# Retention followed by two expert layers on one Trainium2 core: program order on four more queues, decays per chunk, keys scaled on ScalarE

## The chip, the cores and the metric

The kernel runs on one core of a Trainium2 chip. The metric is the device time of one execution in microseconds (us); less is better. A kernel's time is the median of several executions.

## The reference

Retention over 4 batches of 8 heads, 576 positions, head size 64, followed by two dense layers over the 2304 tokens:

```python
scores = scale * np.matmul(q, k.transpose(0, 1, 3, 2))
gamma = 1.0 - 2.0 ** (-5.0 - np.arange(H, dtype=np.float32))
Dmat = np.where(rel >= 0, gamma[:, None, None] ** rel[None, :, :], 0.0)   # rel = query pos - key pos
attn = np.matmul(scores * Dmat[None], v)          # then heads joined: x is 2304 x 512
g = x @ w_gate                                    # 512 x 1536
x = (g * sigmoid(g) * (x @ w_val)) @ w_out        # first layer
h = np.maximum(x @ w_in, 0.0)                     # 512 x 2048
return (h * h) @ w_out2                           # second layer
```

The weights arrive as float64 and are converted on the core.

## The kernel before, in words

**Stage 1, retention.** Two heads make a pair; there are 16 pairs (`pairs`, batch by batch, four a batch). The sequence of a pair is cut into chunks of 128 positions (four whole ones and one of 64). Within a chunk the scores are computed directly (`scores`: matmuls into PSUM tile `s`, then VectorE multiplies them with `mask_sb` into `p_sb`, and for the last short chunk into `pl`). Between chunks a state is carried (`states`: scaled keys times values into PSUM tile `kvs`; ScalarE copies the first chunk's, VectorE adds the other three up, into `sb`). `prep_state` makes the scaled keys in place in `kv_sb` (VectorE for pairs 0 to 3, GpSimd after that) and the scaled queries `qs` (GpSimd). `apply` multiplies states and scores with queries and values into PSUM (`o` for four chunks, a part of the tile `s` for the last), and ScalarE copies that to `xy`. `load` fetches queries and keys (`qk_sb`, three buffers) and values and keys (`kv_sb`, four buffers), and in the first four pairs a quarter each of the mask and of the query decays `qs_sb`.

A loop of 18 steps (n = 0 to 17) runs this as a pipeline: step n computes `scores` and `states` of pair n and, LAG = 2 steps late, `apply` of pair n - 2. The calls stand in the order load(n+2), prep_state(n+1), scores, apply for four chunks, scores of the last chunk, states, one call of `hidden1_early` in steps 6 to 17, apply for the last chunk.

**Work between the steps.** From step 3 on, five calls of `pump` a step advance the conversion of the weights by one piece each. A unit of weights (128 x 512) is loaded as float64 into one of two `raw` buffers (`prefetch`); its five pieces are two ScalarE operations (L161, L162), a clamp (L164), then for the unit before it the split into a high and a low part (`w_hi` on ScalarE, `w_lo` on VectorE, L145 and L146) with a shift (L168), a merge (L170) and an addition (L179). `split_x` cuts 512 columns of `xy` into a high part `xh` (ScalarE) and a low part `xl` (VectorE). `hidden1_early` multiplies the first 512 tokens with one unit (12 matmuls of 512 columns).

**Stage 2** is the rest of both layers: matmuls of 512 columns from `hidden1`, `hidden2`, `out1`, `out2`, three for each product (high x high, high x low, low x high), with the remaining units converted beside them.

**Order.** In stage 1 the matmuls are chained (`tc.issue_after`), so that TensorE runs them in the order of the source. The instructions of VectorE, ScalarE, GpSimd and the DMA triggers on SyncE are put in order by the framework's scheduler, by its own estimate of when each is ready. In stage 2 the scheduler orders all engines.

Of the kernel before, what the change touches and what calls it, by code (L numbers as in the profile page):

```python
# [40 lines left out]
WA = 20  # L41
# [14 lines left out]
def retention_moe_kernel(  # L56
# [34 lines left out]
    chain = {"on": False, "last": None}  # L91

    def matmul(*args, **kw):

        with ExitStack() as behind:
            if chain["on"] and chain["last"] is not None:
                behind.enter_context(tc.issue_after(chain["last"]))
            m = nc.tensor.matmul(*args, **kw)  # L98
        if chain["on"]:
            chain["last"] = m.ins  # L100
        return m
# [10 lines left out]
    def prefetch(upto):  # L112

        while loads["next"] <= min(upto, len(order) - 1):
            i = loads["next"]
            if loads["pool"] < 2:
                loads["pool"] += 1
                raw_flat[i] = raw_p.tile([P, 1024], U32, tag="raw", name="raw")
                raw, back = raw_flat[i].rearrange("p (a n) -> p a n", a=2), None
            elif spare:  # L120
                back = spare.pop(0)
                raw = back.bitcast(U32)
            else:
# [4 lines left out]
            nc.sync.dma_start(out=raw, in_=src.rearrange("p (a n) -> p a n", a=2))  # L128
            raw_t[i] = raw, back
# [12 lines left out]
    def parts_unit(i):  # L142
        wf = w_t.pop(i).bitcast(F32)
        hi, lo = weight_tiles()
        nc.scalar.copy(hi, wf)  # L145
        nc.vector.tensor_tensor(out=lo, in0=wf, in1=f32(hi), op=ALU.subtract)  # L146
        units[order[i]] = (hi, lo)

    def conversion():
        ts = nc.vector.tensor_scalar  # L150
        for i in range(len(order)):
# [9 lines left out]
            nc.scalar.activation(out=low, in_=low16, func=AF.Copy, scale=2.0**-13)  # L161
            nc.scalar.activation(out=wf, in_=high.bitcast(F32), func=AF.Abs)  # L162
# [7 lines left out]
            nc.vector.scalar_tensor_tensor(  # L170
# [7 lines left out]
            for to, lo in adds:  # L178
                nc.vector.tensor_tensor(out=to, in0=to, in1=lo, op=ALU.add)  # L179
# [35 lines left out]
    def split_x(ph, n, cc):  # L215
# [9 lines left out]
        nc.scalar.copy(hi, src)  # L225
        nc.vector.tensor_tensor(out=lo, in0=src, in1=f32(hi), op=ALU.subtract)
        xs[ph, n, cc] = (hi, lo)

    def three(dst, a, b, first, last):
        (ah, al), (bh, bl) = a, b  # L230
        matmul(dst, ah, bh, start=first, stop=False)
        matmul(dst, ah, bl, start=False, stop=False)
        matmul(dst, al, bh, start=False, stop=last)
# [23 lines left out]
    def halves(key, t, early=False):  # L257
# [6 lines left out]
        nc.scalar.copy(hi, t)  # L264
        nc.vector.tensor_tensor(out=lo, in0=t, in1=f32(hi), op=ALU.subtract)  # L265
        hs[key] = (hi, lo)

    def hidden1(n, f, then=None):
# [13 lines left out]
    def hidden1_early(k):  # L282

        f, what = k // 2, "gv"[k % 2]
        if k == 0:
            for cc in range(CC):
                split_x(1, 0, cc)
        (ps,) = project(1, 0, f, (what, what))
        if what == "g":
            early_t[f] = t = t_p.tile([P, 512], F32, tag="t", name="t")  # L290
            nc.scalar.activation(out=t, in_=ps, func=AF.Sigmoid)
        t = early_t[f]
        nc.vector.tensor_tensor(out=t, in0=ps, in1=t, op=ALU.mult)
        if what == "v":
            halves((1, 0, f), early_t.pop(f), early=True)
        if k == 2 * HALF - 1:
            for cc in range(CC):
                split_x(1, 1, cc)

    def hidden2(n, f):  # L300
# [16 lines left out]
    def out1(n, f):  # L317
# [14 lines left out]
        for cc, a in enumerate(acc.pop((1, n))):  # L332
# [5 lines left out]
            if n == 0 and f0:  # L338
                nc.vector.tensor_tensor(out=dst, in0=a[:, :m], in1=dst, op=ALU.add)
            elif cc % 2:  # L340
                nc.vector.tensor_copy(dst, a[:, :m])
            else:
                nc.scalar.copy(dst, a[:, :m])
            if n == 0 and f0 == 0:
                nc.sync.dma_start(out=part[:, cc, :], in_=dst)

    def out2(n, f):
# [7 lines left out]
        if f == F2 - 1:  # L355
            for tt, a in enumerate(acc.pop((2, n))):
# [13 lines left out]
    with ExitStack() as st:  # L370
# [13 lines left out]
        def warm():  # L384

            one = const.tile([P, 256], F32, tag="one", name="one")
            nc.vector.memset(one, 1.0)
            ps = bank("g")
            for _ in range(WARM):
                matmul(ps[:, :256], one[:, :P], one, start=True, stop=True)  # L390

        def load(n):
# [3 lines left out]
            dma = nc.sync.dma_start  # L396
            at = slice(0, CUT) if n == 0 else slice(0, S)
            dma(out=qk_t[n][:, :, at], in_=qk[b, hp][:, :, at])
            if n == 0:
                dma(out=ks_sb, in_=kscale)  # L400
                dma(out=qk_t[n][:, :, CUT:], in_=qk[b, hp][:, :, CUT:])
            dma(out=kv_t[n], in_=kv[b, hp])
            if n < NP:
                dma(out=mask_sb[:, n], in_=mask[:, n])
                dma(out=qs_sb[:, n], in_=qscale[:, n])
# [18 lines left out]
        for x in range(3):  # L424
            nc.gpsimd.memset(p_last[x][S - (NC - 1) * P:], 0.0)

        def scores(n, cs):
# [11 lines left out]
            nc.vector.tensor_tensor(  # L439
# [6 lines left out]
        def states(n):  # L446
# [10 lines left out]
            nc.scalar.copy(sb[:, 0], ps[:, 0])  # L457
            for c in range(1, NC - 1):
                nc.vector.tensor_tensor(out=sb[:, c], in0=ps[:, c], in1=sb[:, c - 1], op=ALU.add)

        def apply(n, last):
# [26 lines left out]
            nc.scalar.copy(xy[:, hp, t0:t0 + bank.shape[-1]], bank)  # L488
# [56 lines left out]
    for ph, n, f, end in steps:  # L545
# [9 lines left out]
        if (ph, n, f) == (1, 0, HALF + 1):  # L555
            nc.sync.dma_start(out=xy[:, :, CHUNKS[1][0][0]:][:, :, :CHUNKS[1][0][1]], in_=part)
# [70 lines left out]
```

## Time and profile before

| | |
|---|---|
| three runs | 951.22, 953.1, 954.19 us; median 953.1 |
| profiled execution | 950.97 us, span 949.2 us |
| mean granted TensorE clock | 0.986 of full speed |
| TensorE busy | 923.5 us, 97% of the span |
| VectorE, ScalarE, GpSimd busy | 469.0, 328.1, 33.7 us |
| moved by DMA | 63.6 MB, mean 67 GB/s |

The span is the time from the first to the last instruction of the profiled execution. Engines are called PE (TensorE), PEld (its weight loads), DVE (VectorE), ACT (ScalarE), POOL (GpSimd), SP (SyncE; SPq its DMA triggers). Because all matmuls go through one helper, they share the line L98, and are told apart by their tiles.

### The profile page before, as it was taken

To read this page: it belongs to the slowest core of one execution; us is meant where nothing else is said; L and a number is where in the kernel's file an instruction comes from. 1 tells how busy PE (TensorE), PEld (TensorE's weight loads), DVE (VectorE), ACT (ScalarE), POOL (GpSimd) and SP (SyncE) were. 2 spreads that over 40 slices of the span, in tenths; PEclk is the share of its full clock that TensorE was granted. 3 is DMA by queue.
4 is the path that set the end of the run, shared out by engine and by line. 5 is a ranking of instruction groups with operands and counts; after the bars stand their busy time and mean duration, and the time that the engine had idled before them with its cause. 6 is when DMAs were issued, how large, how long until landed. Compare 5 with 4: busy or idle time off the path is not lost.

```text
span 949.2 us, 12499 instructions
## 1 busy us (share of the span) xinstructions
PE 923.5 (97%) x5144; PEld 771.5 (81%) x5144; DVE 469.0 (49%) x849; ACT 328.1 (35%) x597; POOL 33.7 (4%) x35
## 2 busy tenths in 40 slices
PE   8499999999999999999999999999999999999998
PEld 6377778788888998888888888888888888888897
DVE  3858667798423332223799888233224222322232
ACT  1443444564312121112566565232223222322232
POOL 2133300000000000000000000000000000000000
PEclk7799999999999999999999999999999999999999
DMA  8756524442100000000244321001001000100010
GB/s 336 248 186 208 197 89 136 137 150 95 60 1 1 2 1 1 1 1 25 69 132 143 122 89 44 1 1 45 1 1 44 1 1 1 45 0 1 1 45 23
DMA packets 22025, 63.60 MB, mean 67 GB/s; under 512 B 2256, under 2 KB 3792, under 8 KB 21968
## 3 DMA queue, kind: packets, MB, share of 16 engines
q1 hardware_dynamic: 21968, 62.81, 19.8%
q8 instruction: 40, 0.66, 0.3%
q14 instruction: 17, 0.14, 0.0%
HBM read 57.03 MB, written 5.77 MB: 66 GB/s over the span
## 4 chain that ended last, share of the span: by engine, by line
PE 81%; DMA 8%; DVE 7%; ACT 2%; issue 1%; SPq 1%; ACTq 0%; DVEq 0%
PE a L98 34%; PE v L98 23%; PE g L98 23%; DMA raw<-in_w 6%; DVE w L170 1%; DVE w L179 1%; DVE w_lo L146 1%; DMA qk_sb<-in_qk 1%; DVE w L164 1%; DMA part<-part_sb 1%; ACT raw L161 1%; DVE p_sb L439 1%; DVE w L168 1%; DVE w_lo L265 0%; ACT w L162 0%
## 5 line engine op out<-in xcount | busy, mean ns | idle before, releaser
L265 DVE TENSOR_TENSOR h_lo<-t,h_hi 128x512 fp32r<-128x512 f32 (+1 forms) x134 | 85.1, 635 | 67.1 <-ACT h_hi L264 66.7
L264 ACT CAST h_hi<-t 128x512 fp32r<-128x512 f32 (+1 forms) x134 | 77.2, 576 | 118.1 <-DVE t L276 64.5
L98 PE MATMUL g<-xh,w_hi 128*128 128x512 f32 (+1 forms) x304 | 114.1, 375 | 0.8 <-ACT xh L225 0.8
L98 PE MATMUL v<-xh,w_hi 128*128 128x512 f32 (+1 forms) x304 | 113.7, 375 | 0.0
L98 PE MATMUL g<-xh,w_lo 128*128 128x512 f32 (+1 forms) x304 | 113.3, 373 | 0.0
L98 PE MATMUL g<-xl,w_hi 128*128 128x512 f32 (+1 forms) x304 | 113.2, 372 | 0.0
L98 PE MATMUL v<-xh,w_lo 128*128 128x512 f32 (+1 forms) x304 | 113.2, 372 | 0.0
L98 PE MATMUL v<-xl,w_hi 128*128 128x512 f32 (+1 forms) x304 | 113.2, 372 | 0.0
L98 PE MATMUL a<-w_lo,h_hi 128*128 128x512 f32 x288 | 112.3, 390 | 0.0
L98 PE MATMUL a<-w_hi,h_hi 128*128 128x512 f32 x288 | 112.2, 390 | 0.0
L98 PE MATMUL a<-w_hi,h_lo 128*128 128x512 f32 x288 | 109.8, 389 | 0.0
L98 PE MATMUL a<-h_lo,w_hi 128*128 128x512 f32 (+1 forms) x216 | 78.9, 366 | 0.0
L98 PE MATMUL a<-h_hi,w_lo 128*128 128x512 f32 (+1 forms) x216 | 78.9, 365 | 0.0
L98 PE MATMUL a<-h_hi,w_hi 128*128 128x512 f32 (+1 forms) x216 | 77.0, 366 | 1.2 <-ACT h_hi L264 1.2
L306 DVE SCALAR_TENSOR_TENSOR t<-g,t 128x512 f32<-128x512 f32 (+1 forms) x40 | 25.5, 637 | 105.5 <-ACT t L304 105.4
L274 DVE TENSOR_TENSOR t<-g,t 128x512 f32<-128x512 f32 (+1 forms) x54 | 34.0, 630 | 85.1 <-ACT t L272 84.8
L306 DVE SCALAR_TENSOR_TENSOR t<-v,t 128x512 f32<-128x512 f32 (+1 forms) x40 | 25.5, 638 | 92.4 <-ACT t L304 92.1
L98 PEld LDWEIGHTS g<-xh,w_hi 128*128 128x128 f32 x304 | 57.2, 188 | 11.5 <-ACT xh L225 1.2
L98 PEld LDWEIGHTS v<-xh,w_hi 128*128 128x128 f32 x304 | 57.3, 188 | 10.3 <-issue 0.2
L98 PEld LDWEIGHTS g<-xh,w_lo 128*128 128x128 f32 x304 | 57.3, 188 | 10.1
L98 PEld LDWEIGHTS v<-xh,w_lo 128*128 128x128 f32 x304 | 57.3, 188 | 10.1
L98 PEld LDWEIGHTS g<-xl,w_hi 128*128 128x128 f32 x304 | 57.3, 188 | 9.8
(88 smaller groups left out, 1486.0 us busy)
## 6 DMA issues: line engine op xcount, KB each, us to landing
raw<-in_w SPq DMA_DIRECT2D x51, 512.0 KB, 3.6
kv_sb<-in_kv SPq DMA_DIRECT2D x16, 576.0 KB, 5.0
xy<-in_w SPq DMA_DIRECT2D x17, 512.0 KB, 3.8
qk_sb<-in_qk SPq DMA_DIRECT2D x15, 576.0 KB, 5.0
out<-o_sb SPq DMA_DIRECT2D x18, 256.0 KB, 2.3
part<-part_sb SPq DMA_DIRECT2D x4, 256.0 KB, 2.8
xy<-part SPq DMA_DIRECT2D x1, 1024.0 KB, 5.3
qs_sb<-in_qscale SPq DMA_DIRECT2D x4, 224.0 KB, 7.4
```

The source lines that it names most:

```text
L98: m = nc.tensor.matmul(*args, **kw)
L146: nc.vector.tensor_tensor(out=lo, in0=wf, in1=f32(hi), op=ALU.subtract)
L161: nc.scalar.activation(out=low, in_=low16, func=AF.Copy, scale=2.0**-13)
L164: ts(out=wf, in0=wf, scalar1=TINY, scalar2=HUGE, op0=ALU.max, op1=ALU.min)
L168: ts(out=w, in0=w, scalar1=3, scalar2=0x3FFFFFFF, op0=ALU.logical_shift_left, op1=ALU.bitwise_and)
L170: nc.vector.scalar_tensor_tensor(out=w, in0=high, scalar=0xC0000000, in1=w, op0=ALU.bitwise_and, op1=ALU.bitwise_or)
L179: nc.vector.tensor_tensor(out=to, in0=to, in1=lo, op=ALU.add)
L264: nc.scalar.copy(hi, t)
L265: nc.vector.tensor_tensor(out=lo, in0=t, in1=f32(hi), op=ALU.subtract)
L274: nc.vector.tensor_tensor(out=t, in0=g, in1=t, op=ALU.mult)
L306: nc.vector.scalar_tensor_tensor(out=t, in0=ps, scalar=0.0, in1=t, op0=ALU.max, op1=ALU.mult)
L439: nc.vector.tensor_tensor(out=pt[:w], in0=ps[:w, :, :nx * w].rearrange("p h (c q) -> p h c q", c=nx), in1=mask_sb[:w, hp, :, None, :w].to_ ...
```

## The change

1. **Order.** A small class `Chained` wraps each of the five engines. While `chain["on"]` holds, that is in stage 1, each instruction on VectorE, ScalarE, GpSimd and each DMA trigger on SyncE is put behind the one before it in the source, as matmuls were already.
2. **The step rewritten.** `load` becomes `load_qk` and `load_kv`. Step n begins with load_kv(n+1) (before: n+2) and load_qk(n+2). `prep_state(n+1)` moves to the end of the step. Two of the five pumps stand together after the main scores (in step 3 only one), and one stands between the last chunk's scores and `states`. `split_x(1, 0, cc)` moves from step 6 to one call in each of steps 3 to 6, between `apply` and the last chunk's scores; `split_x(1, 1, cc)` moves from step 17's `hidden1_early` to after the loop.
3. **Decays per chunk.** Keys are scaled with the decays within one chunk, the same for all chunks; the carried state is multiplied with one decay for each chunk (`scalar_tensor_tensor` in place of `tensor_tensor`). The query decays then repeat too, so `qs_sb` has 161 columns instead of 448, and the GpSimd multiplication is cut into one of 3 x 128 columns and one of 64.
4. **Key scaling on ScalarE**: two `act.mul` of 256 columns a pair with a scale from `ks_sb`, in place of one VectorE or GpSimd multiplication of 512.
5. **WA** goes from 20 to 21: one more weight unit is converted in stage 1 (15 instead of 14).

The core of the diff (all other hunks only replace `nc.vector`, `nc.scalar`, `nc.gpsimd`, `nc.sync` and `matmul` by `dve`, `act`, `pool_e`, `sp` and `pe.matmul`):

```diff
-WA = 20
+WA = 21
...
+        def __getattr__(self, name):
+            op = getattr(self.engine, name)
+
+            def traced(*args, **kw):
+                with ExitStack() as behind:
+                    if chain["on"] and self.last is not None:
+                        behind.enter_context(tc.issue_after(self.last))
+                    i = op(*args, **kw)
+                if chain["on"]:
+                    self.last = i.ins
+                return i
...
+    pe, dve, act, pool_e, sp = map(Chained, (nc.tensor, nc.vector, nc.scalar, nc.gpsimd, nc.sync))
...
-        if k == 0:
-            for cc in range(CC):
-                split_x(1, 0, cc)
...
-        if k == 2 * HALF - 1:
-            for cc in range(CC):
-                split_x(1, 1, cc)
...
-            kn = kv_t[n][:, NC:, :].rearrange("p t (h d) -> p t h d", h=2)
-            (nc.gpsimd if n >= NP else nc.vector).tensor_tensor(
-                out=kn, in0=kn, in1=ks_sb[:, hp].to_broadcast([P, NC - 1, 2, D]), op=ALU.mult
-            )
+            for h, r in enumerate(rs):
+                kn = kv_t[n][:, NC:, r]
+                act.mul(kn, kn, ks_sb[:, hp, 1, h])
             qs = q_p.tile([P, S - P], F32, tag="qs", name="qs")
-            nc.gpsimd.tensor_tensor(
-                out=qs, in0=qk_t[n][:, 0, P:], in1=qs_sb[:, hp, :], op=ALU.mult
-            )
+            for c, m in ((0, 3 * P), (3 * P, D)):
+                w = min(m, P)
+                pool_e.tensor_tensor(
+                    out=qs[:, c:c + m].rearrange("p (c q) -> p c q", q=w),
+                    in0=qk_t[n][:, 0, P + c:P + c + m].rearrange("p (c q) -> p c q", q=w),
+                    in1=qs_sb[:, hp, None, :w].to_broadcast([P, m // w, w]), op=ALU.mult,
+                )
...
-                nc.vector.tensor_tensor(out=sb[:, c], in0=ps[:, c], in1=sb[:, c - 1], op=ALU.add)
+                dve.scalar_tensor_tensor(
+                    out=sb[:, c], in0=sb[:, c - 1], scalar=qs_sb[:, pairs[n][1], -1:], in1=ps[:, c],
+                    op0=ALU.mult, op1=ALU.add,
+                )
...
-        qs_sb = const.tile([P, NP, S - P], F32, tag="qs", name="qs_sb")
-        load(0)
-        load(1)
+
+        qs_sb = const.tile([P, NP, P + D // 2 + 1], F32, tag="qs", name="qs_sb")
+        load_qk(0)
+        load_kv(0)
+        load_qk(1)
         prep_state(0)
...
+            if nxt:
+                load_kv(n + 1)
             if n + 2 <= last:
-                load(n + 2)
+                load_qk(n + 2)
             if n == FROM - 3:
                 prefetch(1)
-            if nxt:
-                prep_state(n + 1)
             if new:
                 scores(n, range(NC - 1))
-            pump(fill)
+            pump(fill if n == FROM - 3 else 2 * fill)
             if old:
                 apply(n - LAG, False)
             pump(fill)
+            if LAG < n <= LAG + CC:
+                split_x(1, 0, n - LAG - 1)
             if new:
                 scores(n, (NC - 1,))
+            pump(fill)
+            if new:
                 states(n)
             pump(fill)
             if FROM <= n < FROM + 2 * HALF:
                 hidden1_early(n - FROM)
-            pump(fill)
             if old:
                 apply(n - LAG, True)
-            pump(fill)
-
+            if nxt:
+                prep_state(n + 1)
+        for cc in range(CC):
+            split_x(1, 1, cc)
     chain["on"] = False
```

## Rows read from the trace of the kernel before

**Rows 1.** The page: busy time of the engines, and one DMA group.

```profile
PE 923.5 (97%) x5144; PEld 771.5 (81%) x5144; DVE 469.0 (49%) x849; ACT 328.1 (35%) x597; POOL 33.7 (4%) x35
...
qs_sb<-in_qscale SPq DMA_DIRECT2D x4, 224.0 KB, 7.4
```

**Rows 2.** Windows by stage: busy us (and instructions) of each engine, clock, DMA share, GB/s.

```profile
4.90:20.82 15.92, 12.54 (x146) 10.44 (x145) 8.32 (x17) 1.63 (x4) 3.40 (x3) 0.68 1.01 389
20.82:32.14 11.32, 4.82 (x77) 3.77 (x73) 8.21 (x18) 5.58 (x12) 2.46 (x3) 0.86 0.76 273
32.14:44.21 12.07, 6.44 (x74) 5.23 (x72) 10.84 (x21) 6.41 (x13) 2.20 (x3) 0.78 0.73 257
...
58.93:66.20 7.27, 7.27 (x89) 5.76 (x85) 3.30 (x7) 1.13 (x4) 2.18 (x3) 1.00 0.51 166
...
137.63:186.00 48.37, 46.41 (x206) 37.80 (x203) 34.81 (x65) 25.42 (x45) 0.00 (x0) 1.00 0.44 134
186.00:944.00 758.00, 757.95 (x3637) 639.78 (x3636) 341.41 (x605) 250.68 (x442) 0.00 (x0) 1.00 0.11 36
```

**Rows 3.** TensorE's waits in the first 270 us: total, times, longest.

```profile
PE s L98 <- DVE pl L439: 10.6, 3, 5.2
...
PE g L98 <- ACT xh L225: 0.8, 1, 0.8
```

**Rows 4.** TensorE in order of time, stage 1: start, us, what.

```profile
25.42 0.69 PE L98 MATMUL kvs<-kv_sb 128*64 128x64 f32 x16 [1.25 <-DVE sb L459]
...
32.14 2.08 PE L98 MATMUL s<-qk_sb 64*128 64x128 f32 x16
...
36.75 0.33 PE L98 MATMUL s<-qk_sb 64*64 64x64 f32 x4
37.67 0.69 PE L98 MATMUL kvs<-kv_sb 128*64 128x64 f32 x16 [0.59 <-issue]
43.40 0.48 PE L98 MATMUL s<-qs,sb 64*64 64x64 f32 x4 [5.04 <-DVE pl L439]
...
58.93 1.16 PE L98 MATMUL s<-qk_sb 64*128 64x128 f32 x16
...
61.85 0.33 PE L98 MATMUL s<-qk_sb 64*64 64x64 f32 x4
```

**Rows 5.** VectorE in order of time, 27 to 31 us.

```profile
27.88 1.22 DVE L439 TENSOR_TENSOR p_sb<-s,mask_sb 128x1024 f32<-128x1024 f32 x1
...
30.99 0.28 DVE L439 TENSOR_TENSOR pl<-s,mask_sb 64x128 f32<-64x128 f32 x1
```

**Rows 6.** SyncE's DMA triggers in order of time.

```profile
14.43 1.78 SPq L128 DMA_DIRECT2D raw<-in_w  x2
...
20.93 0.33 SPq L402 DMA_DIRECT2D kv_sb<-in_kv  x1
```

**Rows 7.** The transfers issued by line L128.

```profile
DMA to landing us min/median/max: 3.1/3.6/7.9
```

**Rows 8.** Groups of instructions, 0 to 145 us: busy, mean ns.

```profile
L410 POOL TENSOR_TENSOR kv_sb<-kv_sb,ks_sb 128x512 f32<-128x512 f32 x12 | 12.9, 1074 | 50.5 <-DMA kv_sb<-in_kv 46.4 <-DVE sb L459 4.2
...
L161 ACT ACTIVATE raw<-raw 128x512 uint32<-128x512 uint16 x17 | 11.4, 673 | 46.4 <-DMA raw<-in_w 42.2 <-DVE p_sb L439 4.2
...
L488 ACT COPY xy<-o 128x512 f32<-128x512 f32 x16 | 9.2, 576 | 9.7 <-PE o L98 9.6
...
L226 DVE TENSOR_TENSOR xl<-xy,xh 128x512 fp32r<-128x512 f32 x8 | 6.1, 770 | 6.3 <-ACT xh L225 6.2
...
L225 ACT CAST xh<-xy 128x512 fp32r<-128x512 f32 x8 | 4.8, 617 | 0.5 <-PE v L98 0.3
...
L457 ACT COPY sb<-kvs 128x64 f32<-128x64 f32 x16 | 3.3, 204 | 12.8 <-PE kvs L98 12.8
L410 DVE TENSOR_TENSOR kv_sb<-kv_sb,ks_sb 128x512 f32<-128x512 f32 x4 | 2.8, 692 | 9.1 <-DMA kv_sb<-in_kv 9.1
```

**Rows 9.** The chain that ended last, one of its pieces: start, us, what.

```profile
192.16 2.72 PE a L98 x12
```

More of the change, by code (lines that the diff above doesn't have):

```diff
@@ L89, in f32, with __init__ @@
         return ap.bitcast(F32)
[L91 to L101, printed above, removed]
+    chain = {"on": False}
+    class Chained:
+        def __init__(self, engine):
+            self.engine, self.last = engine, None
+        def __getattr__(self, name):
[8 more added lines that the diff above has]
+                return i
+            return traced
+    pe, dve, act, pool_e, sp = map(Chained, (nc.tensor, nc.vector, nc.scalar, nc.gpsimd, nc.sync))
     units = {}
@@ L127, in prefetch @@
             src = (w1, w2)[ph - 1][f, :, ("gvo", "io")[ph - 1].index(what), :].bitcast(U32)
-            nc.sync.dma_start(out=raw, in_=src.rearrange("p (a n) -> p a n", a=2))
+            sp.dma_start(out=raw, in_=src.rearrange("p (a n) -> p a n", a=2))
             raw_t[i] = raw, back
@@ L224, in split_x @@
             lo = xs_p.tile([P, N], F32R, tag="xl", name="xl")[:, :m]
-        nc.scalar.copy(hi, src)
-        nc.vector.tensor_tensor(out=lo, in0=src, in1=f32(hi), op=ALU.subtract)
+        act.copy(hi, src)
+        dve.tensor_tensor(out=lo, in0=src, in1=f32(hi), op=ALU.subtract)
         xs[ph, n, cc] = (hi, lo)
@@ L230, in three @@
         (ah, al), (bh, bl) = a, b
-        matmul(dst, ah, bh, start=first, stop=False)
-        matmul(dst, ah, bl, start=False, stop=False)
-        matmul(dst, al, bh, start=False, stop=last)
+        pe.matmul(dst, ah, bh, start=first, stop=False)
+        pe.matmul(dst, ah, bl, start=False, stop=False)
+        pe.matmul(dst, al, bh, start=False, stop=last)
     def cut(pair, a, n):
@@ L263, in halves @@
             lo = h_p.tile([P, N], F32R, tag="hl", name="h_lo")[:, :m]
-        nc.scalar.copy(hi, t)
-        nc.vector.tensor_tensor(out=lo, in0=t, in1=f32(hi), op=ALU.subtract)
+        act.copy(hi, t)
+        dve.tensor_tensor(out=lo, in0=t, in1=f32(hi), op=ALU.subtract)
         hs[key] = (hi, lo)
@@ L338, in out1 @@
             if n == 0 and f0:
-                nc.vector.tensor_tensor(out=dst, in0=a[:, :m], in1=dst, op=ALU.add)
+                dve.tensor_tensor(out=dst, in0=a[:, :m], in1=dst, op=ALU.add)
             elif cc % 2:
-                nc.vector.tensor_copy(dst, a[:, :m])
+                dve.tensor_copy(dst, a[:, :m])
             else:
-                nc.scalar.copy(dst, a[:, :m])
+                act.copy(dst, a[:, :m])
             if n == 0 and f0 == 0:
-                nc.sync.dma_start(out=part[:, cc, :], in_=dst)
+                sp.dma_start(out=part[:, cc, :], in_=dst)
     def out2(n, f):
@@ L386, in warm, with load_qk @@
             one = const.tile([P, 256], F32, tag="one", name="one")
-            nc.vector.memset(one, 1.0)
+            dve.memset(one, 1.0)
             ps = bank("g")
             for _ in range(WARM):
-                matmul(ps[:, :256], one[:, :P], one, start=True, stop=True)
-        def load(n):
+                pe.matmul(ps[:, :256], one[:, :P], one, start=True, stop=True)
+        def load_qk(n):
             b, hp = pairs[n]
             qk_t[n] = qk_p.tile([P, 2, S], F32, tag="qk", name="qk_sb")
-            kv_t[n] = kv_p.tile([P, 2 * NC - 1, P], F32, tag="kv", name="kv_sb")
[L396 to L402, printed above, removed]
+            for at in (slice(0, CUT), slice(CUT, S)) if n == 0 else (slice(0, S),):
+                sp.dma_start(out=qk_t[n][:, :, at], in_=qk[b, hp][:, :, at])
+                if n == 0 and at.start == 0:
+                    sp.dma_start(out=ks_sb, in_=kscale)
@@ L403, in load, with load_kv @@
+        def load_kv(n):
+            b, hp = pairs[n]
+            kv_t[n] = kv_p.tile([P, 2 * NC - 1, P], F32, tag="kv", name="kv_sb")
+            sp.dma_start(out=kv_t[n], in_=kv[b, hp])
             if n < NP:
-                dma(out=mask_sb[:, n], in_=mask[:, n])
-                dma(out=qs_sb[:, n], in_=qscale[:, n])
+                sp.dma_start(out=mask_sb[:, n], in_=mask[:, n])
+                sp.dma_start(out=qs_sb[:, n], in_=qscale[:, n, P:P + qs_sb.shape[-1]])
         def prep_state(n):
@@ L487, in apply @@
             t0 = b * S + cs[0] * P
-            nc.scalar.copy(xy[:, hp, t0:t0 + bank.shape[-1]], bank)
+            act.copy(xy[:, hp, t0:t0 + bank.shape[-1]], bank)
         chain["on"] = True
```

50 lines of the change are left out of this document (25 added, 25 removed).

## The prediction

> **What bounds the kernel now.** I read the page first [rows 1]: TensorE is busy for 923.5 of 949.2 us, so at most 25.7 us can be won by filling its gaps, and something on top where its clock is low. The table of windows by stage says where both lie [rows 2]. From 186 to 944 us TensorE is busy for 757.95 of 758 us at full clock: nothing done to the queues of the first stage can shorten that stretch, and whatever is gained ahead of it moves it forward whole. From 137.63 to 186 it idles for 1.96 us. The gaps are in stage 1, above all in two stretches of 11.32 and 12.07 us with 4.82 and 6.44 us of work and a mean clock of 0.86 and 0.78. By the order of the scores matmuls (4.9 us is step 0, 20.82 step 3, 58.93 step 7) these are steps 3 and 4. A step that also holds a `hidden1_early` call takes 7.27 us with no idle time at all (58.93 to 66.20); 12 matmuls of 512 columns take 2.72 us [rows 9], so a plain warm step would take 4.55.
>
> The table of waits names the cause [rows 3]: 10.6 us in three waits on `pl`, two of them over 5 us. TensorE's timeline [rows 4] shows them after `kvs` of steps 3 and 4: the last chunk's `apply` writes into the tile `s` that VectorE has yet to read for `pl`. On VectorE [rows 5], `p_sb` of step 3 starts at 27.88 and `pl` at 30.99, although their scores were done before 25.42. Ahead of them, and between them, stand weight conversion pieces that wait for ScalarE and for `raw`. So the order in which VectorE's queue was written stops TensorE, not VectorE's load (49% of the span).
>
> **The change, part by part.**
>
> *Order on VectorE.* In source order `p_sb` comes directly behind its scores, and only one piece of a later unit (L179), the clamp of the next unit and, in steps 3 to 6, one `xl` stand ahead of `pl`. The first stall does not go away, though, it changes its cause. The DMA triggers are chained too. In the trace the first two `raw` loads went out at 14.43, ahead of the load of pair 4's keys and values, which had to wait until the last `apply` of step 2 freed a buffer (20.93) [rows 6]. In source order they stand behind that load and behind the queries of pair 5. The clamp in step 3 waits for `raw`, and `pl` stands behind the clamp. That is what comes late next, and I cost it.
>
> Step 3 starts earlier than 20.82: two loads of `qs_sb` that stand ahead of pair 2's queries shrink from 224 to 80 KB [rows 1], 0.29 MB, at 389 GB/s [rows 2] 0.7 us. So 20.1. Then three transfers of 576, 576 and 512 KB, 1.70 MB, take 4.4 us at that rate. A 512 KB load lands 3.6 us after its issue in the median [rows 7], of which 1.35 is moving, so about 2.25 is fixed. The first `raw` lands near 20.1 + 0.1 + 2.25 + 4.4 = 26.8. Behind it come L161 and its equal L162 (0.67 each), the copy to `xy` (0.58), `xh` (0.62), `xl` (0.77) [rows 8] and `pl` (0.28) [rows 5]: 3.6, so 30.4. TensorE was ready at 20.1 + 2.92 (from 58.93 to 61.85) + 0.9 (last scores and `kvs`) = 23.9 [rows 4]. Thus a wait of some 6.5 us remains, ending at 30.4 instead of 31.3, and the clock falls as it did. Bounds of the landing: 3.1 and 7.9 us after issue.
>
> Step 4 starts 0.9 later, at 31.3. Cold, its scores and first `apply` take 36.75 - 32.14 = 4.6 [rows 4]: 35.9. The second long stall has lost its cause, since `raw` 1 landed long before. A short one is left: `xh` is written behind the copy of `apply`, so `pl` is done 0.58 + 0.62 + 0.77 + 0.28 = 2.25 after that `apply`, at 38.1, while TensorE is ready 0.9 to 1.5 after it. Step 5 starts at 38.8; warm, 2.92 + 2.25 + 0.55 = 5.7, so step 6 starts at 44.5, and at 7.27 for that (there the `hidden1_early` call covers the 2.25) step 7 starts at 51.8. Before it was 58.93: **7.1 us** won.
>
> *Steps 7 to 17.* Before: 58.93 to 137.63, 78.7 us. Nine full steps at 7.27 and two without scores and states at 7.27 - 1.97 = 5.3 make 76.0. For this `pl` must be ready when the hidden call ends, 6.6 us into the step; the last scores end 3.2 us into it and `pl`, with one unit a step, about 3.5, and the clamp finds its `raw`, asked for in the step before. **2.7 us** won. Cover: 3 us a step; without it each us late is paid 11 times.
>
> *Stage 2.* One unit more is converted, and in order: nothing of unit 14 is left for the time after the loop but its last addition and its split. Of the 1.96 us idle I take **1 us** as won. The four `split_x(1, 1)` now follow the last `apply`; TensorE waited 0.8 us for them before [rows 3] and will again, or does `out1` meanwhile.
>
> *Key scaling.* Twelve GpSimd multiplications of 1.07 and four on VectorE of 0.69 go, 32 on ScalarE of 256 columns come; each lies between 0.20 (64 columns) and 0.62 (512) [rows 8], I take 0.4. In a step of 7.27 ScalarE has nine operations of 0.2 to 0.67, some 4.3 us, and they stand at the end of a step with `kvs` 3.2 us into the next: hidden, cost 0. If values and keys landed 7.27 + 2 us after their issue they would show. In the Trainium skill, ScalarE: Activation LUTs (Rules for kernel authors) says to use VectorE, not ScalarE, for `mul`, and What ACT_TABLE_LOAD costs there gives 186 + 93 + 0.833 N ns with one pointer operand. By that, as an estimate, 0.49 each and 0.98 a pair against VectorE's 0.69, which would lengthen a queue that has room; the sum stays.
>
> *The rest.* The query scaling in two pieces on GpSimd: nothing waits for it for two steps, 0. The state with one decay more has the same shape as before on VectorE, three short operations, with nothing to 0.3 us a step, hidden. Loading values and keys a pair later: they have one step, 4.55 at the least, and are first needed 3 us into the next one; hidden.
>
> Sum: 7.1 + 2.7 + 1 = 10.8. The profiled execution took 950.97, thus 940.2; the median of the runs is 2.1 above that execution, thus **942 us**.
>
> **The rivals.**
>
> *A. Every step waits for `raw` (slower).* ScalarE's two conversion pieces stand ahead of the copy to `xy`, and VectorE's clamp ahead of `pl`; if `raw` lands late in each step, all behind it on both queues is late, and TensorE stops 14 times. A load asked for 3 us into a step must have landed 8.8 us later. The longest landing is 7.9 and the median 3.6 [rows 7], which speaks against it. From a landing of 9.6 the loss (0.8 in each of 14 steps) eats the gain; at 11 the time is 942 + 14 x 2.2 = 973. The Trainium skill, TensorE: Matmul & The Clock Gate (Architectural detail), calls the queues of ScalarE and VectorE strict first in, first out. The trace agrees: `pl` started at 30.99 with its input 5 us old. 7%.
>
> *B. The gain is eaten by the clock.* Steps 4, 5 and 6 each contain waits of 1 to 2 us behind the long one. If TensorE stays at 1.2 GHz through them, a step's scores and `apply` cost 4.6 instead of 2.9 in step 5, and step 6, 7.27 warm, up to 5 more: some 6.5 us, time 948 to 951. For it: a mean clock of 0.68 in steps 0 to 2 [rows 2], full of short waits. Against it: after the 1.25 us wait at 25.42 the `kvs` group took 0.69 us, no more than at 37.67 after a wait of half that [rows 4]. 14%.
>
> *C. The first stall goes too.* If `raw` lands with 3.1 us and moves beside the other two, `pl` is ready near 27, and steps 4 and 5 lose their short waits: 5 us more, 935 to 937. 10%.
>
> *D. The order comes out as before.* If the scheduler's own order already was the source's, nothing would change. Rows 5 show it was not. What can remain is that stage 2 is ordered anew and gives back what stage 1 wins: 1.96 us idle would have to become 12. 5%, 951 to 955.
>
> **How the numbers follow.** Forecast 64%: 936 to 948. Runs of this kernel lie within 0.3% of each other, and this is what counts as no change, 950.2 to 956.0. Faster: 64 + 10 of C + 5 of B's good half = 79%. Same: 9 of B and 4 of D, 13%. Slower: 7 of A and 1 of D, 8%. The range from 935 (C) to 950 (most of B) leaves out A, D, and the ends of B and C, together under 20%.
>
> **What would show it.** Right: `p_sb` within 0.2 us of its scores in every step; one wait of TensorE on `pl` of 5 to 7 us in step 3 with the first `raw` issued after the load of pair 4's keys and values, two waits of 0.5 to 1.5 behind it, none over 0.5 in steps 7 to 17; scores of step 7 near 52 and the end of stage 1 near 128. Wrong: waits on `pl` with `raw` behind them in later steps (A); a clock under 0.9 from 38 to 52 us (B); no wait over 3 us in stage 1 (C); more than 3 us idle after stage 1 (D).

## The result, and the profile after

The changed kernel takes 943.0 us (median of four runs, 942.15 to 944.61) against 953.4 for the kernel before beside it: ratio 0.990, 95% interval [0.9875, 0.9918]. The forecast was 942, with 935 to 950 as its range. The profiled execution took 942.15 us with a span of 940.4; before, it was 950.97 with 949.2.

The page of the changed kernel, busy time of the engines (before: [rows 1]):

```profile
PE 920.8 (98%) x5144; PEld 769.6 (82%) x5144; DVE 466.3 (50%) x845; ACT 340.9 (36%) x629; POOL 21.3 (2%) x39
```

Almost every instruction now goes through the wrapper, so all carry its line, L106, and are told apart by their tiles. The windows by stage (columns as in [rows 2]), for step 3, steps 4 and 5, steps 7 to 17, and stage 2 in two pieces:

```profile
19.26:30.58 11.32, 4.68 (x77) 3.81 (x73) 4.11 (x11) 3.42 (x8) 1.49 (x3) 0.80 0.57 211
30.58:38.77 8.19, 6.99 (x74) 5.76 (x72) 5.05 (x9) 3.86 (x9) 1.58 (x3) 0.65 0.66 210
38.77:44.50 5.73, 4.39 (x76) 3.62 (x72) 5.35 (x12) 3.90 (x9) 1.30 (x3) 1.00 0.76 251
...
51.77:127.88 76.11, 76.11 (x856) 59.96 (x852) 60.16 (x119) 41.14 (x94) 11.40 (x18) 1.00 0.57 194
127.88:186.00 58.12, 56.44 (x247) 46.41 (x248) 45.75 (x87) 32.00 (x57) 0.00 (x0) 1.00 0.47 145
```

Step 3 is as long as before (11.32 us) and as empty: 4.68 us of matmuls. Step 4 now takes 8.19 us where it took 12.07. In steps 7 to 17 TensorE is busy for 76.11 of 76.11 us. TensorE's waits, totals of the whole trace (before: [rows 3]):

```profile
PE s L106 <- DVE pl L106: 9.2, 3, 6.6
PE kvs L106 <- ACT kv_sb L106: 2.4, 1, 2.4
PE a L106 <- ACT xy L106: 1.5, 1, 1.5
...
PE a L106 <- DVE h_lo L106: 0.5, 1, 0.5
```

There are still three waits on `pl`; only their sizes have changed. TensorE in order of time shows them, and the start of stage 2 (before: [rows 4]):

```profile
29.76 0.48 PE L106 MATMUL s<-qs,sb 64*64 64x64 f32 x4 [6.63 <-DVE pl L106]
30.58 2.08 PE L106 MATMUL s<-qk_sb 64*128 64x128 f32 x16
...
35.96 0.47 PE L106 MATMUL s<-qk_sb 64*64 64x64 f32 x4
...
38.25 0.33 PE L106 MATMUL s<-qs,sb 64*64 64x64 f32 x4 [1.20 <-DVE pl L106]
...
43.98 0.33 PE L106 MATMUL s<-qs,sb 64*64 64x64 f32 x4 [1.34 <-DVE pl L106]
...
51.77 1.16 PE L106 MATMUL s<-qk_sb 64*128 64x128 f32 x16
...
129.43 0.50 PE L106 MATMUL a<-w_hi 128*128 128x512 f32 x1 [1.55 <-ACT xy L106]
```

Step 7 starts at 51.77 (forecast 51.8), before at 58.93. Why step 3 still waits is read from three queues together. SyncE's triggers (before: [rows 6]):

```profile
19.41 0.33 SPq L106 DMA_DIRECT2D kv_sb<-in_kv  x1
19.83 0.38 SPq L106 DMA_DIRECT2D qk_sb<-in_qk  x1
20.26 0.90 SPq L106 DMA_DIRECT2D raw<-in_w  x2
```

ScalarE, the first conversion piece and what stands behind it in step 3, and then the same at the end of stage 1:

```profile
26.51 0.65 ACT L106 ACTIVATE raw<-raw 128x512 uint32<-128x512 uint16 x1 [5.56 <-DMA raw<-in_w]
...
27.62 0.57 ACT L106 COPY xy<-o 128x512 f32<-128x512 f32 x1
28.08 0.62 ACT L106 CAST xh<-xy 128x512 fp32r<-128x512 f32 x1
...
127.52 0.67 ACT L106 ACTIVATE raw<-raw 128x512 uint32<-128x512 uint16 x1 [1.98 <-DMA raw<-in_w]
...
128.65 0.61 ACT L106 CAST w_hi<-t 128x512 fp32r<-128x512 f32 x1
129.15 0.22 ACT L106 COPY xy<-s 128x64 f32<-128x64 f32 x1
```

VectorE in step 3 (before: [rows 5]):

```profile
20.47 1.22 DVE L106 TENSOR_TENSOR p_sb<-s,mask_sb 128x1024 f32<-128x1024 f32 x1 [0.46 <-PE s L106]
27.74 0.43 DVE L106 TENSOR_SCALAR w<-w 128x512 f32<-128x512 f32 x1 [6.05 <-ACT w L106]
28.73 0.69 DVE L106 TENSOR_TENSOR xl<-xy,xh 128x512 fp32r<-128x512 f32 x1 [0.56 <-ACT xh L106]
29.34 0.27 DVE L106 TENSOR_TENSOR pl<-s,mask_sb 64x128 f32<-64x128 f32 x1
```

In step 3 `p_sb` now starts at once, where it started at 27.88 before. But `raw` goes out at 20.26 instead of 14.43, behind the loads of pair 4 and pair 5. ScalarE waits 5.56 us for it, VectorE's clamp 6.05, and `pl` stands behind the clamp. The stall of step 3 has changed its cause and kept its size.

### The profile page after: what moved, and what is told of

Same layout as the page of the kernel before. It is cut to its first block, busy times and chain, and to the rows that moved or that the text cites. A ratio compares the mean times of both kernels' runs of the same rounds, so it can differ in the third digit from the quotient of the medians.

```text
span 940.4 us, 12525 instructions
## 1 busy us (share of the span) xinstructions
PE 920.8 (98%) x5144; PEld 769.6 (82%) x5144; DVE 466.3 (50%) x845; ACT 340.9 (36%) x629; POOL 21.3 (2%) x39
## 3 DMA queue, kind: packets, MB, share of 16 engines
HBM read 56.44 MB, written 5.77 MB: 66 GB/s over the span
## 4 chain that ended last, share of the span: by engine, by line
PE 88%; DMA 5%; DVE 4%; ACT 2%; issue 1%; SPq 0%; ACTq 0%
PE a L106 33%; PE g L106 24%; PE v L106 24%; DMA raw<-in_w 3%; PE s L106 3%; PE o L106 3%; DVE w L106 2%; PE kvs L106 1%; DMA xy<-in_w 1%; DVE w_lo L106 1%; DVE t L106 1%; DMA kv_sb<-in_kv 0%; ACT raw L106 0%; DMA part<-part_sb 0%; DVE xl L106 0%
## 5 line engine op out<-in xcount | busy, mean ns | idle before, releaser
L106 ACT ACTIVATE t<-g 128x512 f32<-128x512 f32 (+1 forms) x100 | 55.4, 554 | 211.8 <-PE g L106 211.6
L106 ACT CAST h_hi<-t 128x512 fp32r<-128x512 f32 (+1 forms) x134 | 77.1, 575 | 119.2 <-DVE t L106 113.6
L106 DVE TENSOR_TENSOR h_lo<-t,h_hi 128x512 fp32r<-128x512 f32 (+1 forms) x134 | 85.2, 636 | 67.1 <-ACT h_hi L106 66.7
L106 PE MATMUL v<-xh,w_hi 128*128 128x512 f32 (+1 forms) x304 | 113.8, 374 | 0.0
L106 PE MATMUL g<-xh,w_hi 128*128 128x512 f32 (+1 forms) x304 | 113.8, 374 | 0.0
L106 PE MATMUL g<-xh,w_lo 128*128 128x512 f32 (+1 forms) x304 | 113.3, 373 | 0.0
L106 PE MATMUL v<-xh,w_lo 128*128 128x512 f32 (+1 forms) x304 | 113.2, 373 | 0.0
L106 PE MATMUL g<-xl,w_hi 128*128 128x512 f32 (+1 forms) x304 | 113.2, 372 | 0.0
L106 PE MATMUL v<-xl,w_hi 128*128 128x512 f32 (+1 forms) x304 | 113.2, 372 | 0.0
L106 PE MATMUL a<-w_lo,h_hi 128*128 128x512 f32 x288 | 112.3, 390 | 0.0
L106 PE MATMUL a<-w_hi,h_hi 128*128 128x512 f32 x288 | 112.2, 390 | 0.0
L106 PE MATMUL a<-w_hi,h_lo 128*128 128x512 f32 x288 | 110.1, 389 | 0.0
L106 DVE TENSOR_TENSOR t<-g,t 128x512 f32<-128x512 f32 (+1 forms) x60 | 38.2, 636 | 89.7 <-ACT t L106 89.6
L106 PE MATMUL a<-h_lo,w_hi 128*128 128x512 f32 (+1 forms) x216 | 79.0, 366 | 0.5 <-DVE h_lo L106 0.5
L106 PE MATMUL a<-h_hi,w_lo 128*128 128x512 f32 (+1 forms) x216 | 78.9, 366 | 0.0
L106 DVE SCALAR_TENSOR_TENSOR t<-g,t 128x512 f32<-128x512 f32 (+1 forms) x40 | 25.5, 639 | 105.6 <-ACT t L106 105.4
L106 PE MATMUL a<-h_hi,w_hi 128*128 128x512 f32 (+1 forms) x216 | 76.8, 367 | 0.1
L106 DVE SCALAR_TENSOR_TENSOR t<-v,t 128x512 f32<-128x512 f32 (+1 forms) x40 | 25.6, 639 | 91.7 <-ACT t L106 91.4
L106 DVE TENSOR_SCALAR w<-w 128x512 f32<-128x512 f32 (+1 forms) x136 | 57.4, 423 | 25.9 <-ACT w L106 24.4
L106 PEld LDWEIGHTS g<-xh,w_hi 128*128 128x128 f32 x304 | 57.3, 188 | 10.4 <-issue 0.2
L106 PEld LDWEIGHTS v<-xh,w_hi 128*128 128x128 f32 x304 | 57.3, 188 | 10.2 <-issue 0.2
L106 PEld LDWEIGHTS v<-xh,w_lo 128*128 128x128 f32 x304 | 57.3, 188 | 10.1
```

The lines of the kernel that those rows point to most:

```text
L106: i = op(*args, **kw)
```

## The experiments

All are compared with the kernel before, run on the same chip. "Step 7" is where the scores of step 7 start in the one profiled execution; in the changed kernel that is 51.77.

| | edit | median us | ratio, 95% interval | step 7 |
|---|---|---|---|---|
| e1 | only TensorE chained | 956.3 | 1.0037 [1.0019, 1.0056] | 59.70 |
| e2 | before, VectorE chained | 957.6 | 1.0049 [1.0030, 1.0067] | 64.03 |
| e9 | ScalarE not chained | 954.6 | 1.0025 [1.0012, 1.0039] | 52.37 |
| e3 | SyncE not chained | 938.9 | 0.9845 [0.9818, 0.9873] | 47.06 |
| e4 | first `raw` asked for in step 2 | 940.0 | 0.9862 [0.9836, 0.9889] | 48.12 |
| e5 | `split_x` ahead of `apply` | 944.0 | 0.9911 [0.9891, 0.9932] | 51.43 |
| e11 | pieces behind `pl` in steps 4, 5 | 944.8 | 0.9928 [0.9910, 0.9947] | 52.29 |
| e6 | e3 and e5 | 936.5 | 0.9850 [0.9822, 0.9877] | 44.04 |
| e12 | e6 and e11 | 937.7 | 0.9844 [0.9823, 0.9865] | 45.53 |
| e7 | e6 and the last `apply` earlier | 936.7 | 0.9835 [0.9821, 0.9850] | 46.14 |
| e8 | keys scaled by GpSimd | 943.9 | 0.9911 [0.9895, 0.9926] | 54.27 |
| e10 | WA = 20 | 941.7 | 0.9894 [0.9876, 0.9912] | 52.11 |

**e1. Is it the order, or the lighter work?** All of the change is kept but the chains of the four engines:

```diff
-    pe, dve, act, pool_e, sp = map(Chained, (nc.tensor, nc.vector, nc.scalar, nc.gpsimd, nc.sync))
+    pe, dve, act, pool_e, sp = Chained(nc.tensor), nc.vector, nc.scalar, nc.gpsimd, nc.sync
```

> The changed kernel with only TensorE chained in stage 1, VectorE, ScalarE, GpSimd and SyncE ordered by the scheduler; source order, decays, key scaling and WA stay. Order theory (the gain comes from running the queues in source order): most of it is lost, 949 to 955 us, with waits on pl of 3 us or more behind conversion pieces. Work theory (the gain comes from lighter work: smaller decay loads, no key scaling on VectorE and GpSimd): it stays, 940 to 945.

956.3 us: the whole gain is gone, and a little more. In its table of TensorE's waits, those on `pl` are back at 11.6 us in five, with 5.4 as the longest (before: 10.6 in three):

```profile
PE s L106 <- DVE pl L449: 11.6, 5, 5.4
```

The gain needs the order. Fewer decays, another engine for the keys and the rewritten step bring nothing without it, taken together. Whether the order would bring the gain in the old step, without the rewritten one, no run tests.

**e2. Is VectorE's order enough?** The kernel before, with `nc.vector` alone put behind the same wrapper:

```diff
+    dve = Chained(nc.vector)
...
-            nc.vector.tensor_tensor(
+            dve.tensor_tensor(
```

> The kernel before with nothing changed but VectorE chained in stage 1 like TensorE. Order theory: VectorE's queue is the one that counts; p_sb and pl come ahead of conversion pieces, the two waits of 5 us shrink to under 3 in all, 939 to 946 us. Work theory: 950 to 955. A third way: the old place of pump and split_x in the step puts pl behind pieces that wait for raw, and the time rises over 956.

The two 5 us waits on `pl` do vanish: five small ones remain, 1.6 us at most. Others come in their place. TensorE's waits, one of VectorE's, and VectorE in step 6:

```profile
PE g L98 <- DVE xl L115: 6.6, 1, 6.6
PE s L98 <- DVE pl L115: 5.4, 5, 1.6
```

```profile
DVE sb L115 <- ACT sb L478: 14.8, 5, 4.2
```

```profile
56.97 0.74 DVE L115 TENSOR_TENSOR sb<-kvs,sb 128x64 f32<-128x64 f32 x3 [3.23 <-ACT sb L478]
...
58.56 2.49 DVE L115 TENSOR_TENSOR xl<-xy,xh 128x512 fp32r<-128x512 f32 x4
```

A chained VectorE stops for whatever ScalarE, still in the scheduler's order, brings late: 14.8 us in five waits for its copy into `sb`. One of them, 3.23 us, stands ahead of the four `xl` that step 6 has before the rewrite, and TensorE waits 6.6 us for these. The time is that of the expectation's third way, but it is not `raw` ahead of `pl` that makes it. Here one ordered queue beside unordered ones is no gain.

**e9. Does ScalarE's order count in the changed kernel?**

```diff
+    pe, dve, pool_e, sp = map(Chained, (nc.tensor, nc.vector, nc.gpsimd, nc.sync))
+    act = nc.scalar
```

> The changed kernel with ScalarE's instructions no longer chained (VectorE, GpSimd, the DMA triggers and TensorE stay chained). Theory that ScalarE's order counts too: with VectorE alone in order, waits of 4.16 and 4.14 us for ScalarE's copy into sb stood in TensorE's and VectorE's rows, so here too some copy, xh or sb written late in ScalarE's queue stops the chained VectorE: 947 to 957 us, with waits on ScalarE over 2 us in stage 1. Rival, that VectorE's order together with the rewritten step is enough, because ScalarE has some 4.3 us of work in a step of 7.27: within 0.3% of the changed kernel's 943, waits on pl as there (6.6, 1.2, 1.3).

954.6 us: without ScalarE's chain nothing of the gain is left. The copy into `sb` does stop VectorE, as was expected: 13.2 us in six waits, the longest 3.82, none of them later than step 7. But step 7 starts only 0.6 us later than in the changed kernel, and no wait of TensorE on ScalarE is over 2 us within steps 3 to 17: most of the loss stands elsewhere. ScalarE in order of time in step 9 with the matmul that waits for it, and then, from the table of waits, what VectorE and TensorE wait for:

```profile
70.91 0.68 ACT L174 ACTIVATE raw<-raw 128x512 uint32<-128x512 uint16 x1 [3.01 <-DMA raw<-in_w]
...
72.52 0.21 ACT L502 COPY xy<-s 128x64 f32<-128x64 f32 x1
...
72.78 0.33 PE L106 MATMUL s<-qk_sb 64*64 64x64 f32 x4 [1.19 <-ACT xy L502]
```

```profile
DVE sb L106 <- ACT sb L468: 13.2, 6, 3.8
...
PE s L106 <- ACT xy L502: 7.0, 8, 1.5
```

The scheduler puts the next unit's conversion, which waits 3.01 us for `raw`, ahead of the copy of the finished `apply`; that copy frees the tile `s`, and the last chunk's scores at 72.78 wait for it. This is rival A's mechanism, and its price: eight waits of 0.15 to 1.5 us, seven of them from step 7 on. Stage 1 ends 8.9 us later than in the changed kernel (136.79 against 127.88), stage 2 takes 2.7 longer, together the 11.6 by which the spans differ (952.0 and 940.4). The Trainium skill, TensorE: Matmul & The Clock Gate (Architectural detail), calls ScalarE's queue strict first in, first out; the copy at 72.52 behind a conversion that waited 3 us agrees.

**e3. Does the chain on the DMA triggers make the first stall?**

```diff
-    pe, dve, act, pool_e, sp = map(Chained, (nc.tensor, nc.vector, nc.scalar, nc.gpsimd, nc.sync))
+    pe, dve, act, pool_e, sp = *map(Chained, (nc.tensor, nc.vector, nc.scalar, nc.gpsimd)), nc.sync
```

> The changed kernel with SyncE left to the scheduler, the other four chained. Trigger theory (the 6.6 us wait of step 3 stands because the first raw load queues behind the load of pair 4's keys and values): raw goes out before 17 us, the wait falls under 2 us, step 4 stays at full clock, 933 to 938 us. Bandwidth theory (the transfers themselves are the limit there): 941 to 945.

938.9 us, some 4 faster than the changed kernel. SyncE's triggers, TensorE's waits, and the windows of steps 3 to 5:

```profile
13.66 1.78 SPq L140 DMA_DIRECT2D raw<-in_w  x2
```

```profile
PE s L106 <- DVE pl L106: 4.0, 3, 1.3
```

```profile
19.48:25.21 5.73, 4.39 (x77) 3.62 (x73) 3.85 (x10) 3.40 (x8) 1.29 (x3) 1.00 1.02 411
25.21:32.50 7.29, 5.95 (x76) 4.92 (x72) 5.25 (x10) 3.99 (x9) 1.71 (x3) 0.77 0.76 240
32.50:39.79 7.29, 5.95 (x76) 4.91 (x72) 5.44 (x12) 3.86 (x9) 1.30 (x3) 0.77 0.74 239
```

`raw` goes out at 13.66, ahead of the load of pair 4 as in the kernel before, and the wait of step 3 falls from 6.63 to 1.34 us. The cause is shown. The gain is less than expected because the clock now falls in steps 4 and 5, to 0.77, after waits no longer than those of the changed kernel: 1.56 us of extra matmul time in each.

**e4. The same by the source's order alone**: all chained, `raw` asked for one step earlier.

```diff
-            if n == FROM - 3:
+            if n == FROM - 4:
                 prefetch(1)
```

> The changed kernel with the first two raw loads asked for in step 2 instead of step 3, all five queues chained. Trigger theory: the wait of step 3 falls from 6.6 to about 1.3 us (the copy to xy, xh, xl and pl behind apply), and step 4 keeps its clock, some 2 us more: 934 to 937 us. Bandwidth theory: pair 3's or 4's data come later instead, 940 to 944.

940.0. The triggers stand at 15.22, but ScalarE's first piece starts only at 23.59, 8.4 us after them. That piece, TensorE's wait of step 3, and the window of the loads:

```profile
23.59 0.65 ACT L106 ACTIVATE raw<-raw 128x512 uint32<-128x512 uint16 x1 [2.47 <-DMA raw<-in_w]
...
26.84 0.48 PE L106 MATMUL s<-qs,sb 64*64 64x64 f32 x4 [4.54 <-DVE pl L106]
```

```profile
10.30:27.00 16.70, 12.16 (x188) 10.21 (x184) 8.29 (x19) 6.47 (x16) 3.53 (x6) 0.83 0.92 361
```

The trigger came 5.0 us earlier and the piece started 2.9 earlier: the rest went to the transfers ahead of it, which keep the 16 DMA engines busy for 92% of that time at 361 GB/s. Here the earlier trigger is worth only what the transfers ahead of it leave. The Trainium skill, DMA: Bandwidth & Descriptors (Where 436 GB/s comes from), gives some 435 GB/s as the ceiling of the ports into SBUF and about 358 as what binds a transfer between HBM and SBUF; the busiest window shown here, 411 in e3, stays below the first but lies above the second, so for these loads the measurement decides.

**e5 and e11. What makes the short waits of steps 4 and 5?** The forecast had `xh` behind ScalarE's copy to `xy`. e5 calls `split_x` ahead of `apply`, e11 instead puts the conversion pieces of these two steps behind `pl`:

```diff
+            if LAG < n <= LAG + CC:
+                split_x(1, 0, n - LAG - 1)
             if old:
                 apply(n - LAG, False)
             pump(fill)
-            if LAG < n <= LAG + CC:
-                split_x(1, 0, n - LAG - 1)
```

```diff
+            early = n in (FROM - 2, FROM - 1)
-            pump(fill if n == FROM - 3 else 2 * fill)
+            pump(0 if early else fill if n == FROM - 3 else 2 * fill)
...
-            pump(fill)
+            pump(0 if early else fill)
...
             if new:
                 scores(n, (NC - 1,))
-            pump(fill)
+            pump(4 * fill if early else fill)
```

> The changed kernel with split_x(1, 0, cc) moved ahead of the apply of four chunks in steps 3 to 6, all five queues chained. If the waits of 1.20 and 1.34 us in steps 4 and 5 come from xh standing behind the copy to xy on ScalarE, they vanish and the wait of step 3 shrinks by some 0.6: 3 us less, 939 to 941. If VectorE's load sets pl there, they stay: 942 to 944.

> The changed kernel with the three conversion pieces that stand ahead of the last chunk's scores in steps 4 and 5 put behind them (split_x stays between apply and those scores). Theory, the copy to xy and xh ahead of xl and pl make the short waits: they stay in both steps at 1.0 to 1.4 us, time 941 to 945. Rival, VectorE's own load makes them: both fall under 0.5 us, time 939 to 941.

Neither helps: 944.0 and 944.8. In e11 the waits are 1.32 and 1.61 us. VectorE in its steps 4 and 5:

```profile
36.87 0.69 DVE L106 TENSOR_TENSOR xl<-xy,xh 128x512 fp32r<-128x512 f32 x1 [3.29 <-ACT xh L106]
...
41.74 1.22 DVE L106 TENSOR_TENSOR p_sb<-s,mask_sb 128x1024 f32<-128x1024 f32 x1
42.87 0.68 DVE L106 TENSOR_TENSOR xl<-xy,xh 128x512 fp32r<-128x512 f32 x1
```

In step 4 no piece stands in front, and `xl` waits for `xh`: the chain copy, `xh`, `xl`, `pl` makes that wait by itself, as forecast. In step 5 `xl` waits for nothing: the pieces moved out of step 4 stand ahead of `p_sb`, and `xl` comes straight behind that. There it is VectorE's queue. In e5 the chain is broken, and the waits become 0.15 and 1.89. The windows of its steps 4 and 5 say why:

```profile
30.56:36.31 5.75, 5.60 (x74) 4.72 (x72) 4.67 (x8) 3.84 (x9) 1.58 (x3) 0.77 0.75 225
36.31:42.60 6.29, 4.40 (x77) 3.62 (x73) 6.22 (x13) 4.02 (x9) 1.54 (x3) 1.00 0.84 278
```

VectorE is busy for 6.22 of 6.29 us in step 5, while TensorE has 4.40 of work. Behind the first cause stands a second one with nearly the same price: a step without a `hidden1_early` call is shorter than VectorE's work in it.

**e6, e12 and e7. Combinations.** e6 is e3 and e5 together. e12 adds e11's edit. e7 is e6 with the last `apply` of steps 16 and 17 ahead of `hidden1_early`:

```diff
+            if not new:
+                apply(n - LAG, True)
             if FROM <= n < FROM + 2 * HALF:
                 hidden1_early(n - FROM)
-            if old:
+            if old and new:
                 apply(n - LAG, True)
```

> The changed kernel with SyncE left to the scheduler and split_x moved ahead of apply. The three waits of 1.34 us go, and with them the two falls of the clock that followed them with SyncE free (steps 4 and 5 took 7.29 us each, 0.77 granted): steps 3, 4 and 5 take 4.5 us each, 7 us less than with SyncE free alone, 931 to 934. If those falls have nothing to do with the waits: 934 to 937.

> DMA triggers not chained, split_x ahead of apply, and the three conversion pieces of steps 4 and 5 behind the last chunk's scores. If both things together make the short waits (the copy and xh ahead of xl in step 4, VectorE's load in step 5), neither is left in steps 4 and 5: waits on pl there under 0.5 us each, only that of step 3 stays (1.8), 933 to 936 us. Rival, that a third thing holds pl there (the load of raw, or p_sb late behind the pieces that were moved): a wait of 1 us or more in step 4 or 5, or a new wait on p_sb or sb, 936 to 940 us.

> As the run with SyncE free and split_x first, and in steps 16 and 17 the last apply stands ahead of the hidden1_early call, so that its copy on ScalarE is not behind the pieces of the next weight unit. The wait of 1.5 to 1.7 us at the start of stage 2 goes: 1.5 us less, and 1.5 more if the clock fell there: 928 to 932. If another wait takes its place: as without it.

e6 is the fastest median, 936.5, 1.5% under the kernel before; e12 and e7 can't be told from it. The waits on `pl` that were to go in e6 are still there, 1.79, 1.98 and 0.94 us in steps 3 to 5, but in its profile the clock does not fall behind them. In e12 the waits of steps 4 and 5 are 0.54 and 1.76, and that of step 3 grows to 2.92; the rival came true there. Its step 5 (columns as above):

```profile
30.55:36.70 6.15, 4.39 (x77) 3.61 (x73) 6.03 (x12) 3.97 (x11) 1.30 (x3) 1.00 0.96 317
```

6.03 of 6.15 us again. Over steps 4 and 5 together the waits on `pl` come to 2.5 us in the changed kernel (1.20 + 1.34), 2.0 in e5, 2.9 in e11, 2.9 in e6 and 2.3 in e12: these edits only move them. e7 does away with the wait on `xy` at the start of stage 2, but its waits on `h_hi` (1.5 us) and `h_lo` (1.0) take its place, so that nothing is won.

**e8 and e10. The two small parts.** e8 lets GpSimd scale the keys; e10 sets WA back.

```diff
-            for h, r in enumerate(rs):
-                kn = kv_t[n][:, NC:, r]
-                act.mul(kn, kn, ks_sb[:, hp, 1, h])
+            kn = kv_t[n][:, NC:, :].rearrange("p t (h d) -> p t h d", h=2)
+            pool_e.tensor_tensor(
+                out=kn, in0=kn, in1=ks_sb[:, hp, 1, None].to_broadcast([P, NC - 1, 2, D]), op=ALU.mult
+            )
```

```diff
-WA = 21
+WA = 20
```

> The changed kernel with the keys of all pairs scaled by one GpSimd multiplication of 512 columns in place of two on ScalarE; order, decays and loads stay. Order theory: no change within 0.3%, since neither engine is waited for after step 0: 941 to 945. Work theory (ScalarE's scaling carries a part of the gain, by VectorE's slower operations beside GpSimd): 945 to 950.

> The changed kernel with WA back at 20 (one weight unit less converted in stage 1, all else as changed). Theory that the order of the queues makes the time: within 0.3% of 943, 941 to 945; the waits of steps 3 to 5 stay (6.6, 1.2, 1.3), and stage 2 takes the same within 1 us, since what it waits for at its start is the copy into xy and not a weight. Rival, that one unit more is a part of the gain (the forecast's 1 us in stage 2): 944 to 947, with a wait on w_hi or w_lo back at the start of stage 2.

943.9 and 941.7: both within 0.3% of the changed kernel by their ratios. In e10 the wait at the start of stage 2 is still on `xy` (1.85 us), not on a weight. Its profile has no wait on `h_lo` and a stage 2 that is 1.1 us shorter; whether the further unit costs that much the medians can't tell. Neither part carries any of the gain that can be measured.

## Why the prediction was right, and where it was off

*Up to step 7: forecast 7.1 us, measured 7.16* (58.93 to 51.77). Step by step: `pl` of step 3, forecast for 30.4, was done at 29.6, since `raw` landed near 26.5 instead of 26.8 and each operation behind it started some 0.1 us before the end of the last; a wait of about 6.5 us is 6.63; step 4 at 31.3 is 30.58, step 5 at 38.8 is 38.77, step 6 at 44.5 is 44.50.

That the last ones fit so closely is luck, since errors cancel. Step 3 starts at 19.26, not 20.1 (TensorE's waits on `qk_sb` ahead of it, 2.0 us in three before, are gone from the table). The first `raw` trigger then comes 1.0 us after that start, not 0.1, because the triggers ahead of it follow each other some 0.4 us apart. Step 4 starts 0.7 early and takes 8.19 where 7.5 was forecast: its scores and first `apply` stay slow for 5.4 us (30.58 to 35.96), not 4.6.

e3 shows that the cause of the remaining stall, the chained trigger, was the right one: it costs some 4 us of the median. The two short waits were put between 0.5 and 1.5 and measure 1.20 and 1.34. Their mechanism was half of the truth: e11 confirms the chain behind the copy in step 4; in step 5 e5, e11 and e12 show VectorE's load right behind it.

*Steps 7 to 17: forecast 2.7, measured 2.6* (78.70 to 76.11), at 7.27 a full step with no wait; `pl` starts 3.3 to 3.8 us into steps 7 to 15 (forecast: about 3.5). e9 shows that this needs ScalarE's order, which keeps the last chunk's copy to `xy` ahead of the next unit. The longest wait of the same stretch before, 1.16 us, was on that copy too.

*Stage 2: forecast 1 us won, measured 1.0 lost.* This is the term that was mis-sized. From the last `apply` to the end it took 811.57 us before (949.2 - 137.63) and takes 812.52 (940.4 - 127.88). I took one of the 1.96 us of idle time as won because a further unit was converted in order. The idle time stayed: 1.68 us up to 186 (58.12 - 56.44) and 0.50 at 207.93 for `h_lo`, 2.18 in all; before, next to none came after 186. The scheduler, which orders stage 2, now begins with `a`, whose pool is opened, by the code, once those of stage 1 are closed, and the table of waits has it wait for the copy out of `s`. That copy (129.15) stands behind unit 15's conversion, which belongs to stage 2 and waited 1.98 us for `raw`. TensorE idles 1.55 us there; e10 has the same wait without the further unit. So of the 0.95 lost only 0.2 is added idle time of the matmuls. The last output transfer took 0.5 us more to finish (3.7 us from its first trigger to the end of the span before, 4.2 now), and TensorE is busy 0.2 us longer (805.64 for 805.43); for these two I have no cause.

*The sum*: 7.16 + 2.6 - 0.95 = 8.8 against 10.8, and the profiled executions differ by 8.82. The median still came within 1 us of the forecast because that execution lies 0.85 us under its median, not 2.1 as the one before did; that part was luck.

*Key scaling*: 0.4 us each was taken, 0.50 measured in the mean of 32. The Trainium skill's figure (ScalarE: Activation LUTs, What ACT_TABLE_LOAD costs), by which 0.49 was estimated, was the better one. It is hidden but in one place, which I had not costed: `kvs` of step 0 waits 2.4 us for it, where it waited 1.3 for VectorE's scaling before. ScalarE first loads a table there:

```profile
7.40 1.28 ACT L106 ACT_TABLE_LOAD   x1 [7.40 <-DMA kv_sb<-in_kv]
```

*The rivals.* A did not come in the changed kernel, but e9 shows its mechanism at work as soon as ScalarE loses its order. (The input of `pl` at 30.99, called 5 us old there, was 6.8 us old: its scores ended at 24.17.) One sign failed: `p_sb` was to start within 0.2 us of its scores in every step, and starts some 0.6 behind them in steps 5, 6, 8, 10, 12 and 14, though no wait of TensorE names it. B did not come: clock 1.00 in steps 5 and 6. It did in the profiles of e3, e5, e7, e8, e10 and e12, where one or two of steps 4 to 6 took some 1.6 us more. C is e3: the stall that didn't go away does, for less than the 5 us put on it. D came in a small way, 1 us given back. In e9 it gave back another 2.7.

## What to carry to other kernels

An engine that waits for a tile whose inputs are long done points at the queue of the engine that writes it, not at that engine's load. In this kernel, ordering such queues by hand paid only for the compute engines together: VectorE's alone brought nothing (e2), and ScalarE's left out undid the gain (e9). VectorE or GpSimd left out alone was not tested. DMA triggers are the exception to look at first: a trigger that waits for a free buffer, in a queue that keeps its order, holds up every load behind it.

## What the runs showed of the hardware

TensorE's clock does not follow from the length of a wait alone. At the same place, the start of stage 2, e6 waited 1.65 us and e12 1.49. TensorE in order of time, e6 and then e12:

```profile
121.80 0.50 PE L106 MATMUL a<-w_hi 128*128 128x512 f32 x1 [1.65 <-ACT xy L106]
...
124.08 0.63 PE L106 MATMUL a<-w_hi 128*128 128x512 f32 x1
```

```profile
123.13 0.50 PE L106 MATMUL a<-w_hi 128*128 128x512 f32 x1 [1.49 <-ACT xy L106]
...
124.62 0.40 PE L106 MATMUL a<-w_hi 128*128 128x512 f32 x1
```

In e6 the same matmuls go over to 0.63 us (1.2 GHz; the mean clock of the 10 us from 119.82 is 0.83), in e12 they stay at 0.40 (2.4 GHz). After a wait of 2.92 us in step 3 of e12 the scores took 1.16, at full clock, and after 1.62 in e7 they took 2.08. In these runs such a fall costs about 1.6 us when it hits a step, and that is of the size of the differences between e6, e7 and e12, which is why they can't be ranked.
